# A hand-ordered attention and expert-MLP kernel: eight late W2 rows joined to scores or reads, W2 quads in one row, and another written order

## The chip, the cores and the metric

The kernel runs on one core of one Trainium2 chip. The metric is the device time of one execution in microseconds (us), lower is better. A profile holds the span from the first to the last instruction of one execution. TensorE is PE in the views (its weight loads are PEld), VectorE is DVE, ScalarE is ACT, GpSimd is POOL and SyncE is SP.

## The reference

```python
# x [8,8,512,64], state [8,8,32,64], w_in [512,2048], w_out [2048,512]
scores  = scale * x @ state.T          # softmax over the 32 state rows
xread   = softmax(scores)  @ state     # [8,8,512,64]
scores2 = scale * state @ x.T          # softmax over the 512 tokens
sread   = softmax(scores2) @ x         # [8,8,32,64]
t   = concat([xread, sread], axis=2) -> [8 * 544, 512]
h   = maximum(t @ w_in, 0)
out = (h * h) @ w_out                  # [4352, 512]
```

The two weights arrive as 64-bit floating-point words and are turned into 32-bit numbers on the chip. The result has fp32 accuracy: each large product is three matmuls of split operands (high times high, low times high, high times low).

## The kernel before, in words

**Blocks.** The output has nine blocks: blocks 0 to 7 are the 512 tokens of each batch's x-read, block 8 is the 256 state tokens. For a batch b, `xread @ w_in` is not formed in two steps. The product state times w_in is made first ("W2"; two batches make a "pair", four a "quad") and then multiplied with the softmax numerators.

**Making W2.** w_in is cut into eight column blocks hb of 256 columns. `decode_wi` decodes a column block into `wf{hb}` (two DVE `TENSOR_SCALAR` and four `SCALAR_TENSOR_TENSOR` a half, partly on other engines), `prep_wo` decodes w_out (tiles `dec`, `wo`). `direct_w2` (line 890) makes the pair of batches 0 and 1, `later_w2` (line 927) the quad of batches 2 to 5 in four PSUM banks (`w4ps`, 24 matmuls in two halves of 12), and `last_w2` (line 957) the pair of batches 6 and 7 (`w2ps{hb}_6`, 16 matmuls through `two_w2`). The results are copied out of PSUM (`w4o`, or `w2h` by ACT and `w2l` by DVE), stored to DRAM and loaded again by `load_w2` when their block comes.

**The MLP.** `hidden.blk.fc` ("H blk_fc", 16 fc a block) is six 128x512 matmuls into one of two PSUM banks with the tag `ph`, then relu and square, then the split into `g_hi` (ACT) and `g_lo` (DVE). `accumulate.blk.fc` is twelve matmuls into four banks `acc`. PSUM has four pools of this kind: `acc` with four banks, `ph` with two, `psb` with two.

**Attention.** `scores` makes the 32x512 scores of a batch (`st`, 8 matmuls), `transposes` the numerators `eT` of the state read (`pt`), `sread` the state read (`pr`, 32 matmuls) and its copies. W2 pairs and scores use tiles of 64 rows by 32 columns of the PE array, reads tiles of 128 by 32, quads tiles of 64 by 128; the MLP uses the whole array. `in_a_row` (line 554) issues a list of such matmuls one behind the other: "a row".

**Order.** `PLAN` (lines 24 to 357) is a long string of step names, written by hand. The loop at line 1273 walks through it; each mention of a step runs its generator up to the next `yield`. Every instruction is kept in program order on its engine, SP's DMA queue included, so the string sets the order of each engine. A second table, which the change leaves alone, sets which engine does a piece of evacuation. All instructions go through one helper, so that line 403 stands for all of them in the views.

## Time and profile before

| quantity | value |
|---|---|
| three timed runs | 665.65, 666.88, 665.60 us; median 665.65 |
| span of the profiled execution | 663.4 us |
| its own time over the span | runs less the span: 2.25 us at the median |
| granted TensorE clock | 1.000 in every slice |
| PE matmul busy | 648.4 us, 98% |
| PE weight load busy (beside the matmuls) | 518.3 us, 78% |
| DVE busy | 363.9 us, 55% |
| ACT busy | 358.6 us, 54% |
| POOL busy | 100.3 us, 15% |
| DMA | 102.49 MB, mean 154 GB/s |

The busy share of PE counts a matmul from its start to a modelled end, so neighbouring records overlap by some tenths of a microsecond. What a matmul costs is therefore read from the distance of the starts, not from its length.

### The profile page before, as it was taken

To read this page: it belongs to the slowest core of one execution; us is meant where nothing else is said; L and a number is where in the kernel's file an instruction comes from. 1 tells how busy PE (TensorE), PEld (TensorE's weight loads), DVE (VectorE), ACT (ScalarE), POOL (GpSimd) and SP (SyncE) were. 2 spreads that over 40 slices of the span, in tenths; PEclk is the share of its full clock that TensorE was granted. 3 is DMA by queue.
4 is the path that set the end of the run, shared out by engine and by line. 5 is a ranking of instruction groups with operands and counts; after the bars stand their busy time and mean duration, and the time that the engine had idled before them with its cause. 6 is when DMAs were issued, how large, how long until landed. Compare 5 with 4: busy or idle time off the path is not lost.

```text
span 663.4 us, 10898 instructions
## 1 busy us (share of the span) xinstructions
PE 648.4 (98%) x4132; PEld 518.3 (78%) x4132; DVE 363.9 (55%) x657; ACT 358.6 (54%) x691; POOL 100.3 (15%) x82
## 2 busy tenths in 40 slices
PE   5999999999999999999999999999999999999997
PEld 4667777777788778778777878788778888888886
DVE  5999999866754465445553553446552443212212
ACT  4977776665645565454553645453354455434432
POOL 1521121140330202001301400030001000200100
PEclk9999999999999999999999999999999999999999
DMA  9948787979375566746248045530392227121002
GB/s 312 323 142 235 254 280 244 256 210 278 109 237 168 161 195 215 192 134 161 66 121 226 16 116 146 160 106 32 112 275 68 87 66 187 34 96 33 32 1 95
DMA packets 116276, 102.49 MB, mean 154 GB/s; under 512 B 59520, under 2 KB 92544, under 8 KB 116224
## 3 DMA queue, kind: packets, MB, share of 16 engines
q1 hardware_dynamic: 115984, 101.54, 51.2%
q8 instruction: 32, 0.52, 0.3%
q10 hardware_dynamic: 240, 0.26, 0.1%
q14 instruction: 20, 0.16, 0.1%
HBM read 67.70 MB, written 34.08 MB: 153 GB/s over the span
## 4 chain that ended last, share of the span: by engine, by line
PE 83%; DVE 8%; ACT 3%; DMA 3%; issue 2%; SPq 1%; ACTq 0%
PE acc L403 50%; PE ph L403 26%; DVE wf L403 2%; PE w2ps L403 2%; DVE dec L403 2%; PE w4ps L403 1%; PE st L403 1%; PE pr L403 1%; PE pt L403 1%; ACT ph L403 1%; SPq L403 1%; DMA part<-part_d 1%; DMA wi_raw<-in_moe_w_in_dram 1%; DVE s L403 1%; DVE g_lo L403 1%
## 5 line engine op out<-in xcount | busy, mean ns | idle before, releaser
L403 PE MATMUL acc<-wo,g_hi 128*128 128x512 f32 x1090 | 323.7, 392 | 0.6 <-ACT g_hi L403 0.6
L403 PEld LDWEIGHTS acc<-wo,g_hi 128*128 128x128 f32 x1090 | 201.4, 188 | 49.4 <-issue 4.6
L403 PE MATMUL acc<-wo,g_lo 128*128 128x512 f32 x545 | 197.0, 390 | 0.0
L403 DVE TENSOR_TENSOR g_lo<-ph,g_hi 128x512 fp32r<-128x512 f32 (+1 forms) x143 | 93.4, 657 | 160.5 <-ACT g_hi L403 159.4
L403 PE MATMUL ph<-k_hi,w 128*128 128x512 f32 x512 | 176.6, 395 | 0.5 <-ACT w4o L403 0.2
L403 ACT ACTIVATE ph<-ph 128x512 f32<-128x512 f32 (+1 forms) x194 | 108.4, 560 | 126.7 <-PE ph L403 118.6
L403 PEld LDWEIGHTS acc<-wo,g_lo 128*128 128x128 f32 x545 | 101.9, 188 | 23.2 <-issue 1.2
L403 PEld LDWEIGHTS ph<-k_hi,w 128*128 128x128 f32 x512 | 96.1, 188 | 26.6 <-issue 3.3
L403 PE MATMUL ph<-k_lo,w 128*128 128x512 f32 x256 | 99.8, 390 | 0.0
L403 ACT CAST g_hi<-ph 128x512 fp32r<-128x512 f32 (+1 forms) x144 | 80.4, 564 | 35.1 <-DVE ph L403 30.4
L403 DVE SCALAR_TENSOR_TENSOR ph<-ph,r 128x512 f32<-128x512 f32 (+1 forms) x47 | 31.3, 668 | 55.9 <-ACT r L403 55.9
L403 ACT ACTIVATE r<-ph 128x512 f32<-128x512 f32 (+1 forms) x47 | 27.1, 578 | 61.2 <-PE ph L403 61.1
L403 PEld LDWEIGHTS ph<-k_lo,w 128*128 128x128 f32 x256 | 48.1, 188 | 9.1
L403 POOL TENSOR_TENSOR w<-w_f,w 128x512 fp32r<-128x512 f32 x21 | 27.1, 1294 | 173.4 <-ACT w L403 173.2
L403 POOL TENSOR_TENSOR s<-sf,s 128x512 fp32r<-128x512 f32 x9 | 11.5, 1291 | 111.0 <-ACT s L403 53.5
L403 ACT CAST w<-w_f 128x512 fp32r<-128x512 f32 x40 | 24.8, 624 | 4.0 <-DMA w_f<-w_d 4.0
L403 PE MATMUL ph<-sr_hi,s 128*128 128x256 f32 x128 | 25.4, 282 | 0.0
L403 POOL TENSOR_TENSOR sp<-sp,s 128x512 f32<-128x512 f32 x11 | 11.5, 1050 | 91.0 <-DVE s L403 45.9
L403 DVE SCALAR_TENSOR_TENSOR dec<-wo_raw,dec 128x512 uint32<-128x512 uint32 x32 | 22.9, 719 | 0.7
L403 DVE SCALAR_TENSOR_TENSOR wf<-wi_raw,wf 128x512 uint32<-128x512 uint32 x32 | 22.2, 696 | 0.7
L403 POOL TENSOR_TENSOR wo<-dec,wo 128x512 fp32r<-128x512 f32 x10 | 13.5, 1349 | 57.9 <-ACT wo L403 57.9
L403 PEld LDWEIGHTS ph<-sr_hi,s 128*128 128x128 f32 x128 | 20.9, 191 | 0.6
(111 smaller groups left out, 569.6 us busy)
## 6 DMA issues: line engine op xcount, KB each, us to landing
w_f<-w_d SPq DMA_DIRECT2D x40, 256.0 KB, 3.8
wi_raw<-in_moe_w_in_dram SPq DMA_DIRECT2D x16, 512.0 KB, 5.1
wo_raw<-in_moe_w_out_dram SPq DMA_DIRECT2D x16, 512.0 KB, 6.5
wf<-win_f SPq DMA_DIRECT2D x16, 512.0 KB, 4.6
xr<-in_x_dram SPq DMA_DIRECT2D x16, 512.0 KB, 5.5
w_d<-w4o SPq DMA_DIRECT2D x32, 256.0 KB, 2.5
w<-w2a_d SPq DMA_DIRECT2D x16, 512.0 KB, 3.6
out_dram<-o SPq DMA_DIRECT2D x31, 256.0 KB, 2.8
```

The lines of the kernel that those rows point to most:

```text
L403: op = call(*args, **kw)
```

## The change

Matmuls, copies, DMAs and their engines are the same in number. What changes is in which row a matmul stands and in which order the steps are written.

- `sread` is cut into `read` (its matmuls) and `sread` (its copies). `scores`, `read` and `two_w2` now give back their lists of matmuls, and `together` issues one or two lists as one row.
- The eight late W2 pairs (batches 6 and 7) have no row of their own any more. Five stand ahead of scores in one row (`shared`: batch 3 with hb 1, 4 with 0, 5 with 2, 6 with 3, 7 with 4), with W2 in the two `ph` banks and the scores in `psb`. Three stand ahead of a state read (`beside`: batch 4 with hb 5, 5 with 6, 6 with 7), with W2 in `psb` and the read in one `ph` bank.
- `later_w2` issues its 24 matmuls as one row. In the order before, the two halves of 12 already stood back to back for seven of the eight hb; for hb 2 an accumulate stood between them.
- `PLAN` is written anew from end to end (2215 mentions before, 2199 now).

```diff
+    def together(*names):
+
+        def issue():
+            in_a_row([call for name in names for call in rows[name]()])
+
+        return issue
...
         def scores(self):
...
-            in_a_row(calls)
+            return calls
...
-        def sread(self):
+        def read(self, pool, tag):
...
-            pr = ps_b.tile([P, G, D], F32, tag="psb", name=f"pr{b}")
+            pr = self.pr = pool.tile([P, G, D], F32, tag=tag, name=f"pr{b}")
...
-            in_a_row(calls)
+            return calls
+
+        def sread(self):
+
+            b, pr = self.b, self.pr
...
-    def two_w2(hb, b0, last):
+    def two_w2(hb, b0, pool, tag):
...
-        pool, tag = (ps_h, "ph") if hb == 0 < b0 else (ps_b, "psb")
...
-        in_a_row(calls)
-        return ps
+        return calls
...
     def later_w2(hb):
...
-        ps = []
+        ps, calls = [], []
         for k, (pool, tag) in enumerate(pools):
-            if k:
-                yield
...
-            calls = []
...
-            in_a_row(calls)
             ps += two
+        in_a_row(calls)
...
     def last_w2(hb):
 
-        ps = two_w2(hb, 6, True)
+        ps = w2_ps[hb, 6]
...
+    shared = {3: 1, 4: 0, 5: 2, 6: 3, 7: 4}
+    beside = {4: 5, 5: 6, 6: 7}
+    w2_row = {hb: key("scores", b) for b, hb in shared.items()} | {hb: key("read", b) for b, hb in beside.items()}
...
+        names = [key("scores", b)]
+        if b in shared:
+            names.insert(0, key("w2", shared[b]))
+            needs.append(key("load_wf", 2, shared[b]))
+        step(key("scores", b), together(*names), after=needs)
```

The new order moves steps everywhere. Three places of it follow. A row names the output tile, the inputs and the size; "x2" stands for two in a line.

**First place: the end of the decoding, on DVE and on PE.** DVE before, from the split of H1_7 (`g_lo1_7`) to behind that of H1_6 (`g_lo1_6`); `dec` and `wf` are decodes of w_out and w_in:

```order
L403 TENSOR_TENSOR g_lo1_7_1167<-ph1_7_1155,g_hi1_7_1166 128x512
L403 TENSOR_TENSOR w2_0_4_1115<-w2_f0_4_1116,w2_0_4_1115 128x2x256
L403 TENSOR_SCALAR dec12_1206<-dec12_1206 128x512 x2
L403 SCALAR_TENSOR_TENSOR dec12_1206<-wo_raw12_853,dec12_1206 128x512 x2
L403 COPY w2o6_0_0_1245<-w2ps6_0_0_1227 128x512
L403 TENSOR_TENSOR g_lo1_6_1219<-ph1_6_1187,g_hi1_6_1218 128x512
L403 TENSOR_SCALAR wf7_1250<-wf7_1250 128x512 x2
L403 SCALAR_TENSOR_TENSOR wf7_1250<-wi_raw14_1153,wf7_1250 128x512 x2
```

DVE now, over the same stretch:

```order
L396 SCALAR_TENSOR_TENSOR dec12_1175<-wo_raw12_823,dec12_1175 128x512
L396 TENSOR_TENSOR g_lo1_7_1205<-ph1_7_1197,g_hi1_7_1204 128x512
L396 SCALAR_TENSOR_TENSOR wf7_1173<-wi_raw14_1130,wf7_1173 128x512
L396 TENSOR_TENSOR w2_0_4_1179<-w2_f0_4_1180,w2_0_4_1179 128x2x256
L396 COPY w2o6_0_0_1270<-w2ps6_0_0_1252 128x512
L396 SCALAR_TENSOR_TENSOR dec12_1175<-wo_raw12_823,dec12_1175 128x512
L396 SCALAR_TENSOR_TENSOR wf7_1173<-wi_raw14_1130,wf7_1173 128x512
L396 TENSOR_TENSOR w2_0_5_1190<-w2_f0_5_1191,w2_0_5_1190 128x2x256
L396 TENSOR_TENSOR g_lo1_6_1244<-ph1_6_1182,g_hi1_6_1243 128x512
```

Of all DVE instructions, 169 stand up to and with `g_lo1_6` before and 180 now. The eleven added ones are two `SCALAR_TENSOR_TENSOR` and two `TENSOR_SCALAR` each of `dec10` and of `wf7`, the max `m21_0` with its small `nb21_0`, and the split `w2_0_5`; none is taken out.

PE before, ahead of H0_8 (`ph0_8`), with the last of the accumulates of block 1:

```order
L403 MATMUL acc1_4_3_1197<-wo7_1053,g_hi1_7_1166 128x512 x2
L403 MATMUL acc1_4_0_1194<-wo7_1053,g_lo1_7_1167 128x512
L403 MATMUL acc1_4_1_1195<-wo7_1053,g_lo1_7_1167 128x512
L403 MATMUL acc1_4_2_1196<-wo7_1053,g_lo1_7_1167 128x512
L403 MATMUL acc1_4_3_1197<-wo7_1053,g_lo1_7_1167 128x512
L403 MATMUL ph0_8_1314<-k_hi0_130,w2_0_4_1115 128x512
L403 MATMUL ph0_8_1314<-k_lo0_131,w2_0_4_1115 128x512
```

PE now; the last matmul of the read of batch 0 (`pr0`) stands first:

```order
L396 MATMUL pr0_1289<-xr0_1_1208,eT0_1150 32x64 x2
L396 MATMUL acc1_4_0_1213<-wo5_768,g_lo1_5_1095 128x512
L396 MATMUL acc1_4_1_1214<-wo5_768,g_lo1_5_1095 128x512
L396 MATMUL acc1_4_2_1215<-wo5_768,g_lo1_5_1095 128x512
L396 MATMUL acc1_4_3_1216<-wo5_768,g_lo1_5_1095 128x512
L396 MATMUL ph0_8_1342<-k_hi0_122,w2_0_4_1179 128x512
L396 MATMUL ph0_8_1342<-k_lo0_123,w2_0_4_1179 128x512
L396 MATMUL ph0_8_1342<-k_hi0_122,w2_0_4_1179 128x512 x2
L396 MATMUL ph0_8_1342<-k_lo0_123,w2_0_4_1179 128x512
L396 MATMUL ph0_8_1342<-k_hi0_122,w2_0_4_1179 128x512
L396 MATMUL acc1_4_0_1213<-wo6_905,g_hi1_6_1243 128x512 x2
```

The accumulates with `wo6` and `wo7` (24 matmuls) stood ahead of H0_8 and stand behind it now. H0_9 (six matmuls) and the row `pr0` stood behind it and stand ahead of it now. H0_8 writes the PSUM bank that `g_lo1_6` reads.

**Second place: the pair of hb 1, on PE.** Before, behind the end of the quad of hb 7 (`w4ps7`); the pair itself stands behind H2_12, some 45 rows later:

```order
L403 MATMUL w4ps7_1_0_2719<-wf_hi7_2664,s42_1417 128x256
L403 MATMUL w4ps7_1_1_2720<-wf_hi7_2664,s42_1417 128x256
L403 MATMUL acc2_0_0_2343<-wo8_1058,g_hi2_8_2712 128x512 x2
L403 MATMUL acc2_0_0_2343<-wo8_1058,g_lo2_8_2713 128x512
L403 MATMUL acc2_0_1_2344<-wo8_1058,g_hi2_8_2712 128x512 x2
L403 MATMUL acc2_0_1_2344<-wo8_1058,g_lo2_8_2713 128x512
L403 MATMUL acc2_0_2_2345<-wo8_1058,g_hi2_8_2712 128x512 x2
L403 MATMUL acc2_0_2_2345<-wo8_1058,g_lo2_8_2713 128x512
L403 MATMUL acc2_0_3_2346<-wo8_1058,g_hi2_8_2712 128x512 x2
L403 MATMUL acc2_0_3_2346<-wo8_1058,g_lo2_8_2713 128x512
L403 MATMUL st3_1_2762<-xT3_1_2536,sT_111 32x512
```

Now the first two of the pair's 16 matmuls follow at once (the scores `st3` and then `acc2` with `wo8` follow the sixteenth):

```order
L396 MATMUL w4ps7_1_0_2723<-wf7_1_2534,s46_1545 128x256
L396 MATMUL w4ps7_1_1_2724<-wf7_1_2534,s46_1545 128x256
L396 MATMUL w4ps7_1_0_2723<-wf_hi7_2604,s42_1546 128x256
L396 MATMUL w4ps7_1_1_2724<-wf_hi7_2604,s42_1546 128x256
L396 MATMUL w2ps1_6_1_2765<-wf1_2_2712,sT_111 32x256
L396 MATMUL w2ps1_6_0_2764<-wf1_2_2712,sT_111 32x256
```

The pair writes the two `ph` banks in which the quad's last two tiles stand, so it needs their copies `w4o7_2` (DVE) and `w4o7_3` (ACT).

**Third place: H6_4, on PE.** Before, behind the accumulate of fc 2 and the transposes `pt6`:

```order
L403 MATMUL acc6_0_3_5220<-wo2_555,g_hi6_2_5199 128x512 x2
L403 MATMUL acc6_0_3_5220<-wo2_555,g_lo6_2_5200 128x512
L403 MATMUL pt6_0_5295<-ident_73,e26_4713 128x128 x4
L403 MATMUL pt6_1_5313<-ident_73,e26_4713 128x128 x4
L403 MATMUL ph6_4_5330<-k_hi6_3848,w2_6_2_5072 128x512
```

Now, behind the pair of hb 4 and the scores of batch 7:

```order
L396 MATMUL w2ps4_6_1_5231<-wf4_2_5187,sT_111 32x256
L396 MATMUL w2ps4_6_0_5230<-wf4_2_5187,sT_111 32x256
L396 MATMUL st7_1_5233<-xT7_1_4902,sT_111 32x512
L396 MATMUL st7_0_5232<-xT7_1_4902,sT_111 32x512
L396 MATMUL st7_1_5233<-xT7_1_4902,sT_111 32x512
L396 MATMUL st7_0_5232<-xT7_1_4902,sT_111 32x512
L396 MATMUL st7_1_5233<-xT7_0_4698,sT_111 32x512
L396 MATMUL st7_0_5232<-xT7_0_4698,sT_111 32x512
L396 MATMUL st7_1_5233<-xT7_0_4698,sT_111 32x512
L396 MATMUL st7_0_5232<-xT7_0_4698,sT_111 32x512
L396 MATMUL ph6_4_5264<-k_hi6_3461,w2_6_2_5007 128x512
L396 MATMUL ph6_4_5264<-k_lo6_3462,w2_6_2_5007 128x512
```

The pair stood alone in block 4 before, with an accumulate behind it. H6_4 now writes the bank of `w2ps4_6_0`, which ACT (`w2h`) and then DVE (`w2l`) have to copy out first. The other six shared rows have an accumulate of twelve matmuls behind them.

## Rows read from the trace of the kernel before

**Rows 1.** The page: busy time of the engines.
```profile
PE 648.4 (98%) x4132; PEld 518.3 (78%) x4132; DVE 363.9 (55%) x657; ACT 358.6 (54%) x691; POOL 100.3 (15%) x82
```

**Rows 2.** Busy time by stretches: length, PE, PEld, DVE, ACT, POOL, clock, DMA share, GB/s.
```profile
0.00:24.00 24.00, 16.21 (x176) 12.05 (x176) 16.35 (x31) 14.66 (x30) 6.06 (x9) 1.00 0.94 335
24.00:60.00 36.00, 34.30 (x214) 26.08 (x208) 35.47 (x67) 30.30 (x59) 11.29 (x8) 1.00 0.64 193
60.00:98.00 38.00, 37.12 (x274) 28.28 (x273) 36.99 (x74) 28.21 (x55) 6.99 (x4) 1.00 0.80 266
```

**Rows 3.** PE's timeline round a W2 pair alone: start, length, operation, count.
```profile
241.04 0.39 PE L403 MATMUL ph<-k_hi,w 128*128 128x512 f32 x1
241.36 1.09 PE L403 MATMUL w2ps<-wf,sT 64*32 64x256 f32 x32
242.38 0.73 PE L403 MATMUL acc<-wo,g_hi 128*128 128x512 f32 x2
242.96 0.39 PE L403 MATMUL acc<-wo,g_lo 128*128 128x512 f32 x1
```

**Rows 4.** PE's timeline: a row of scores alone, and a row of a read alone.
```profile
230.58 1.09 PE L403 MATMUL st<-xT,sT 64*32 64x512 f32 x16
...
266.62 1.10 PE L403 MATMUL pr<-xr,eT 128*32 128x64 f32 x64
```

**Rows 5.** PE's timeline: the second half of hb 2's quad alone, then hb 5's 24 in one.
```profile
153.24 0.39 PE L403 MATMUL w4ps<-wf_hi,s 64*128 64x256 f32 x2
...
154.14 2.14 PE L403 MATMUL acc<-wo,g_hi 128*128 128x512 f32 x8
...
226.02 0.39 PE L403 MATMUL w4ps<-wf_hi,s 64*128 64x256 f32 x2
...
227.64 0.73 PE L403 MATMUL acc<-wo,g_hi 128*128 128x512 f32 x2
```

**Rows 6.** Copies out of PSUM: ACT and PE behind a quad, then groups by line.
```profile
217.64 0.73 PE L403 MATMUL acc<-wo,g_hi 128*128 128x512 f32 x2
...
217.74 1.57 ACT L403 COPY w4o<-w4ps 128x512 f32<-128x512 f32 x3 [1.63 <-PE w4ps L403]
...
L403 DVE COPY w4o<-w4ps 128x512 f32<-128x512 f32 x17 | 11.5, 687 | 6.3 <-PE w4ps L403 3.7 <-DMA out_dram<-o 1.3 <-DMA w_d<-w4o 1.1
...
L403 ACT CAST w2h<-w2ps 128x512 fp32r<-128x512 f32 x16 | 8.7, 597 | 4.2 <-PE w2ps L403 4.2
...
L403 DVE TENSOR_TENSOR w2l<-w2ps,w2h 128x512 fp32r<-128x512 f32 x16 | 10.6, 678 | 3.3 <-ACT w2h L403 3.3
```

**Rows 7.** PE's timeline up to H0_8 (the row at 103.94).
```profile
98.50 1.98 PE L403 MATMUL acc<-wo,g_hi 128*128 128x512 f32 x8
...
101.22 1.98 PE L403 MATMUL acc<-wo,g_hi 128*128 128x512 f32 x8
...
103.94 0.39 PE L403 MATMUL ph<-k_hi,w 128*128 128x512 f32 x1
```

**Rows 8.** DVE's timeline over the same time; the row at 97.91 is g_lo1_6.
```profile
95.06 0.88 DVE L403 TENSOR_SCALAR dec<-dec 128x512 f32<-128x512 f32 x2
95.98 1.42 DVE L403 SCALAR_TENSOR_TENSOR dec<-wo_raw,dec 128x512 uint32<-128x512 uint32 x2
97.31 0.68 DVE L403 COPY w2o<-w2ps 128x512 f32<-128x512 f32 x1
97.91 0.68 DVE L403 TENSOR_TENSOR g_lo<-ph,g_hi 128x512 fp32r<-128x512 f32 x1
```

**Rows 9.** PE's timeline: the last of four late waits, behind an accumulate.
```profile
171.34 1.20 PE L403 MATMUL acc<-wo,g_lo 128*128 128x512 f32 x4
172.72 0.50 PE L403 MATMUL ph<-k_hi,w 128*128 128x512 f32 x1 [0.19 <-ACT w4o L403]
```

**Rows 10.** DMA issues of the W2 pairs: count, KB each, us to landing.
```profile
w<-w2a_d SPq DMA_DIRECT2D x16, 512.0 KB, 3.6
w2a_d<-w2h SPq DMA_DIRECT2D x16, 256.0 KB, 2.3
```

More of the change, by code (lines that the diff above doesn't have):

```diff
@@ new lines @@
+    hidden.3.8 softmax.4.1 softmax.4.0 hidden.3.8 hidden.3.8 exp_s.4.0
+    hidden.3.7 hidden.3.8 hidden.3.8 exp_s.4.1 hidden.3.7 hidden.3.8 accumulate.3.5 exp_s.4.0 load_w2.3.5
+        hidden.3.7
+    hidden.3.6 hidden.3.7 softmax.4.1 load_w2.3.7 softmax.4.0 read.3 hidden.3.7 hidden.3.6 hidden.3.7
+        start.6
+    hidden.3.9 hidden.3.6 softmax.4.1 hidden.3.6 load_w2.3.7 load_w2.4.0 load_w2.3.6 hidden.3.9 hidden.3.6
+        hidden.3.6 accumulate.3.6 softmax.4.0
+    hidden.3.11 hidden.3.9 load.5.1 hidden.3.11 accumulate.3.7 hidden.3.9 softmax.4.1 hidden.3.9 load_wf.2.3
+        hidden.3.9 softmax.4.1
@@ L357 @@
+    hidden.8.15 accumulate.7.15 accumulate.7.15 hidden.8.15
+    hidden.8.14 accumulate.7.15 accumulate.7.15 accumulate.8.12 hidden.8.14 accumulate.8.13 accumulate.7.15
+        hidden.8.14 accumulate.7.15 hidden.8.14 hidden.8.15 hidden.8.14 hidden.8.15 hidden.8.15 hidden.8.14
+        hidden.8.15 accumulate.7.15 accumulate.8.14 accumulate.8.15 accumulate.8.13 accumulate.8.14
+        accumulate.8.15 accumulate.8.15 accumulate.8.15 accumulate.8.15 accumulate.8.15
 """
@@ L877, in hi_lo @@
         return w[:, :, 0], w[:, :, 1]
-    def two_w2(hb, b0, last):
-        w = (wf.pop(hb) if last else wf[hb]).bitcast(F32)
-        pool, tag = (ps_h, "ph") if hb == 0 < b0 else (ps_b, "psb")
-        ps = [pool.tile([P, 2, HB], F32, tag=tag, name=f"w2ps{hb}_{b0}_{g}") for g in range(G)]
+    w2_ps = {}
+    def two_w2(hb, b0, pool, tag):
+        w = wf.pop(hb).bitcast(F32)
+        ps = w2_ps[hb, b0] = [pool.tile([P, 2, HB], F32, tag=tag, name=f"w2ps{hb}_{b0}_{g}") for g in range(G)]
         calls = []
@@ L1198, in tile_attn_moe @@
         step(key("warm", i), warm, i, after=["ident"])
+    shared = {3: 1, 4: 0, 5: 2, 6: 3, 7: 4}
+    beside = {4: 5, 5: 6, 6: 7}
+    w2_row = {hb: key("scores", b) for b, hb in shared.items()} | {hb: key("read", b) for b, hb in beside.items()}
+    for b in range(B):
+        rows[key("scores", b)] = lambda b=b: att[b].scores()
+        rows[key("read", b)] = lambda b=b: att[b].read(*((ps_h, "ph") if b in beside else (ps_b, "psb")))
+    for hb in range(NHB):
+        pool = (ps_b, "psb") if hb in beside.values() else (ps_h, "ph")
+        rows[key("w2", hb)] = partial(two_w2, hb, NB + 2, *pool)
     for b in range(B):
@@ L1206, in tile_attn_moe @@
         step(key("load", b, 1), lambda b: att[b].load(1), b, after=[key("start", b)])
-        step(
-            key("scores", b), lambda b: att[b].scores(), b,
-            after=[key("prep", b, 0), key("prep", b, 1), key("states", 0 if early else 2)],
-        )
-        step(
-            key("sread", b), lambda b: att[b].sread(), b,
-            after=[key("transposes", b)] + [key("load_n", b, g) for g in range(G)],
-        )
+        needs = [key("prep", b, 0), key("prep", b, 1), key("states", 0 if early else 2)]
+        names = [key("scores", b)]
[3 more added lines that the diff above has]
+        step(key("scores", b), together(*names), after=needs)
+        names = [key("read", b)]
+        needs = [key("transposes", b)] + [key("load_n", b, g) for g in range(G)]
+        if b in beside:
+            names.insert(0, key("w2", beside[b]))
+            needs += [key("load_wf", 2, beside[b]), key("states", 2)]
+        step(key("read", b), together(*names), after=needs)
+        step(key("sread", b), lambda b: att[b].sread(), b, after=[key("read", b)])
         step(
@@ L1245, in tile_attn_moe @@
         step(key("later_w2", hb), later_w2, hb, after=[key("split_wf", hb), "split_states"])
-        step(key("last_w2", hb), last_w2, hb, after=[made if hb < NOW else key("load_wf", 2, hb), key("states", 2)])
+        step(key("last_w2", hb), last_w2, hb, after=[w2_row[hb]])
     for fc in range(NFC):
```

662 lines of the change are left out of this document (320 added, 342 removed).

## The prediction

> **What bounds the kernel now.** I read the busy times first, then the stretches, then PE's timeline row by row. PE is busy for 648.4 of 663.4 us [rows 1], so a change can win only by shortening PE's work, or its idle 15 us. The stretches show where another engine is near: from 24 to 98 us DVE is busy for 35.47 of 36.00 and 36.99 of 38.00 us [rows 2], and so has 1.5 us to spare in 74. There the decoding of the weights runs on DVE, and PE waits for DVE where the order asks too early. Behind 98 us PE is the only full engine. In the first 24 us neither is full and the DMA share is 0.94 [rows 2].
>
> PE's timeline shows what a short row of small tiles costs. Twelve whole-array matmuls go from 98.50 to 101.22 [rows 7], 0.227 us each. The matmul ahead of a lone W2 pair has 0.32 us until the row starts, and behind the row two matmuls take 0.58 us in place of 0.45 [rows 3]. So the two edges cost 0.09 + 0.13, say 0.2 us, beside the row's own 1.02 us (241.36 to 242.38). Scores and reads alone are rows of the same length [rows 4].
>
> **The change part by part.** The sum is made against the span of 663.4 us. The median of the runs, 665.65, lies 2.25 above it, and I keep that distance. A difference of 0.2% is 1.33 us, about what a measurement of this kernel can tell from no change.
>
> *a, five pairs joined to scores.* A joined row saves one pair of edges, 0.2 us. It also saves the running empty of one row: the quad's half of 12 takes 0.90 us (153.24 to 154.14), but 24 in one take 1.62 (226.02 to 227.64), which is 0.18 less than two halves [rows 5]. The pair and the scores use the same tile shape, 64 by 32 [rows 3, 4], like the quad's two halves. So each saves 0.38 and the five save 1.9 us. If only the edges go it is 1.0; these are the bounds, and I take 1.9 because the quad is the same case.
>
> *b, three pairs joined to reads.* The read's tiles are 128 by 32 [rows 4], so the array goes from one tile shape to another inside the row, and no row of the trace shows that. Bounds: nothing saved, or 0.38 each as with equal shapes, 1.14 in all. I take half, 0.57, since one of the two changes to and from the whole array goes in any case. The Trainium skill, TensorEngine Tiling (Array Packing), section Key Properties, says that a change of tiling mode, as against a change of tile, drains TensorE. By that rule each of the three keeps a drain inside its row, about 0.19 saved each; without it the sum would be 0.57 lower. The trace's edges of 0.2 us between whole array and tiles agree with it.
>
> *c, the quad of hb 2 in one row.* Two rows of 0.90 with edges become one of 1.62 [rows 5]: 0.38 saved. The other seven stood back to back already, so nothing changes for them.
>
> *d, the pair of hb 1 behind the quad of hb 7.* It writes the banks of the quad's last tiles. ACT starts 0.10 us behind the end of a quad (217.64 to 217.74), DVE's copy `w4o` takes 0.69 and ACT's runs beside it [rows 6]: a wait of 0.79. One pair of edges more goes, since quad, pair and scores are now one stretch of tiles: +0.59 net. Bounds 0.4 (with a copy as short as ACT's 0.60) and 1.3 (DVE still has a split of 0.68 ahead [rows 8]). Queued behind the waiting pair are the scores of batch 3 and all of block 2, so the wait counts in full.
>
> *e, H6_4 behind the pair of hb 4 and the scores of batch 7.* The bank is free after the pair (1.02), the start of ACT (0.10), `w2h` (0.60) and `w2l` (0.68) [rows 3, 6]: 2.40 us from the row's start. The row itself is done after 2 × 1.02 less 0.18, with its first edge 0.09: 1.95. H6_4 waits 0.45 us. Bounds 0.3 (the pair's last tile is done 0.18 earlier inside a joined row) and 0.8 (DVE late by part of a split). Behind the other six rows (hb 1 too) an accumulate of 12 × 0.227 = 2.72 us [rows 7] covers the chain of 1.5 us of copies, and I cost them at nothing. If that cover failed, each would pay about 0.45. The stores and loads of this pair (2.3 and 3.6 us to landing [rows 10]) with the copies are some 8.4 us, and until H6_8 PE has four hidden and three accumulates, 4 × 1.36 + 3 × 2.72 = 13.6 us: hidden.
>
> *f, the end of the decoding.* H0_8 started at 103.94 [rows 7]. Ahead of it 24 matmuls go (5.44 us), and six (1.36) and the read of batch 0 (1.02 and 0.2 of edges) come: PE would be there at 101.1. It needs the bank that `g_lo1_6` reads. That split ended at 97.91 + 0.68 = 98.59 [rows 8], 5.3 us ahead of need. Eleven DVE instructions now come ahead of it. A group of two `TENSOR_SCALAR` and two `SCALAR_TENSOR_TENSOR` takes 2.25 us (95.06 to 97.31), and a single operation of this size 0.60 (97.31 to 97.91) [rows 8]. Two groups, the max and the split `w2_0_5` make 4.5 + 1.2 = 5.7, the small `nb21_0` 0.2 more: 5.9. DVE has at most 1.5 us of idle time to put them in [rows 2], so `g_lo1_6` ends between 98.59 + 5.9 − 1.5 = 103.0 and 104.5, or from 102.6 if the operations overlap better. H0_8 waits 1.5 to 3.4 us, and 3.7 if an operation more is late; I take 2.3, near the middle of the first two. Behind H0_8 wait the accumulates of block 1 and all else on PE.
>
> Part of it comes back. PE then runs later against the copies and loads, and it has small late waits to lose: four places, the last one at 171.34, where four matmuls take 1.38 in place of 0.91 us, with ACT's copy named [rows 9]. The four are at 129, 136, 140 and 171 us and cost 1.67 us in all. I take two thirds, 1.1, because the order there is new too and may put others in their place. So f is +1.2, with bounds of −0.2 (1.5 less 1.67) and +3.7.
>
> *The start.* SP issues the second block of w_in third and not eighth. Such a transfer is 512 KB, and at 335 GB/s [rows 2] it is 1.5 us that could move states and x by that much, up or down. The first hidden needs both, so I take nothing, with 0.7 to either side.
>
> Sum: −1.9 − 0.57 − 0.38 + 0.59 + 0.45 + 1.2 = −0.61. The span becomes 662.8 and the time 665.0 us.
>
> **The rivals.**
>
> *Faster: the decoding doesn't bind.* The new order as a whole may use DVE's idle time and give all late waits back. Then f is −0.2, and if the reads join as well as the scores, b is −1.14: −1.9 − 1.14 − 0.38 + 0.59 + 0.45 − 0.2 = −2.58, so 663.1 us. For it: four real waits stand behind 100 us [rows 9], and PE's savings are sure in sign. Against it: eleven more DVE instructions ahead of one that PE needs sooner.
>
> *Slower: DVE's order decides.* All eleven operations are paid, H0_8 waits 3.7 us and nothing comes back: −0.61 − 1.2 + 3.7 = +1.89, so 667.5 us. The terms without f make −1.81, so the kernel is slower by over 1.33 us once f is above 3.1: when `g_lo1_6` ends after 101.1 + 3.1 = 104.2 us and the waits at 129 to 171 us stay. For it: DVE is 98% busy up to 98 us [rows 2]. Against it: nearly the whole of the wait must stay to outweigh 2.85 us of savings.
>
> *Slower: the copies bind.* If the two copies of a pair are late behind every joined row, the seven other rows pay 0.45 each: −0.61 + 3.15 = +2.54, so 668.2. Against it: 2.72 us of accumulate cover 1.5 us of copies. The Trainium skill, the same page, section PSUM Bottleneck, warns that tiling speeds TensorE but not the evacuation of PSUM, so that the copies may become the limit. By that rule the time would be this rival's; the trace shows it only where no accumulate follows.
>
> *The rows don't gain.* Joining saves edges only, reads nothing: −1.0 − 0.38 + 0.59 + 0.45 + 1.2 = +0.86, so 666.5 us, within 0.2%.
>
> **How the numbers follow.** Forecast 0.38, faster rival 0.35, DVE's order 0.17, the copies 0.04, no gain in the rows 0.06. The forecast and the last are within 0.2%: 0.44. Faster 0.35, slower 0.21. The range goes from the faster rival to the slower one, 663.1 to 667.5, with 0.2 at either side for the start: 662.9 to 667.7. The copies and the far ends of the start and of d are left out. The forecast's own range, with d, e and f varied by half their bounds, is 664.1 to 666.4.
>
> **What would show it.** In the profile after: joined rows of pair and scores, 1.86 us from their start to the next matmul, and pair and read 1.86 to 2.04; a wait of PE of about 0.8 us behind the quad of hb 7, named for `w4o`; about 0.45 ahead of H6_4, named for `w2l`; between 99 and 106 us a wait of PE for a `g_lo` of 1.5 to 3.4. If H0_8 doesn't wait, f is wrong. If the waits near 129 to 171 us stand as before, so is the give-back. If joined rows take 2.04 and more, a is wrong. If the first hidden moves by over 0.7 us, the start was mis-costed.

## The result and the profile after

The changed kernel takes 674.85 us (median of four runs, 673.20 to 675.47) against 665.91 for the kernel before (four runs): a ratio of 1.0126 with the 95% interval 1.0111 to 1.0141. It is slower by 8.9 us, where 0.6 less was forecast, and lies 7 us above the range. The profiled execution is the run of 675.47 us with a span of 673.7.

The page's busy times after, which answer to [rows 1]:

```profile
PE 651.5 (97%) x4132; PEld 522.4 (78%) x4132; DVE 360.7 (54%) x657; ACT 356.6 (53%) x691; POOL 102.7 (15%) x82
```

The work is the same. The span of the profiled executions grew by 10.3 us, and in it PE is idle for 7.2 us more and busy for 3.1 more. The stretches after, with the columns of [rows 2], say where:

```profile
24.00:60.00 36.00, 33.85 (x230) 24.66 (x229) 34.57 (x67) 27.53 (x54) 9.69 (x7) 0.95 0.55 162
...
98.00:160.00 62.00, 59.48 (x407) 46.26 (x408) 45.76 (x80) 38.17 (x72) 14.52 (x10) 1.00 0.85 255
...
233.00:245.00 12.00, 9.01 (x89) 5.29 (x88) 4.92 (x8) 3.70 (x7) 0.50 (x1) 0.86 0.76 248
```

For the middle one the kernel before had:

```profile
98.00:160.00 62.00, 61.71 (x409) 48.11 (x416) 48.66 (x84) 41.50 (x78) 14.68 (x11) 1.00 0.84 246
```

Two stretches show something that was in none of the forecast's terms: the granted clock is 0.95 in 24 to 60 us and 0.86 in 233 to 245, where the kernel before had 1.00 all along. In 24 to 60 us PE loses only some tenths of busy time against [rows 2], so there the lower clock matters as well as the idle time. In 98 to 160 PE is idle for 2.5 us, 0.3 before. PE's waits name what was late (after; us in total, times, longest):

```profile
PE w2ps L396 <- DMA wf<-win_f: 3.0, 1, 3.0
PE w2ps L396 <- DVE sp L396: 1.9, 1, 1.9
PE ph L396 <- DVE g_lo L396: 1.6, 2, 1.2
PE pr L396 <- DMA xr<-in_x_dram: 1.4, 2, 1.0
PE w4ps L396 <- DVE g_lo L396: 0.8, 1, 0.8
```

The largest of these, and the largest new one (the wait for x in the first microseconds is 4.3 us, 3.6 before), is a load, that of column block 1 for the W2 pair of batches 6 and 7. PE's timeline after shows its place and the other rows that the forecast spoke of: the wait at the second W2 pair (34.07), H0_8 (106.93), H0_12 (123.60), the joined row of hb 1 (238.90 and 240.75), a pair with scores (434.02), a pair with a read (486.06) and H6_4 (504.33):

```profile
34.07 2.55 PE L396 MATMUL w2ps<-wf,sD 64*32 64x256 f32 x32 [1.95 <-DVE sp L396]
...
106.93 0.39 PE L396 MATMUL ph<-k_hi,w 128*128 128x512 f32 x1
...
123.60 0.50 PE L396 MATMUL ph<-k_hi,w 128*128 128x512 f32 x1 [1.19 <-DVE g_lo L396]
...
235.62 0.28 PE L396 MATMUL w4ps<-wf_hi,s 64*128 64x256 f32 x2
238.90 1.96 PE L396 MATMUL w2ps<-wf,sT 64*32 64x256 f32 x32 [3.00 <-DMA wf<-win_f]
240.75 1.84 PE L396 MATMUL st<-xT,sT 64*32 64x512 f32 x16
242.52 0.74 PE L396 MATMUL acc<-wo,g_hi 128*128 128x512 f32 x2
...
434.02 1.09 PE L396 MATMUL w2ps<-wf,sT 64*32 64x256 f32 x32
434.90 1.06 PE L396 MATMUL st<-xT,sT 64*32 64x512 f32 x16
435.90 0.73 PE L396 MATMUL acc<-wo,g_hi 128*128 128x512 f32 x2
...
486.06 1.09 PE L396 MATMUL w2ps<-wf,sT 64*32 64x256 f32 x32
487.08 1.10 PE L396 MATMUL pr<-xr,eT 128*32 128x64 f32 x64
488.11 0.50 PE L396 MATMUL ph<-k_hi,w 128*128 128x512 f32 x1
...
504.33 0.50 PE L396 MATMUL ph<-k_hi,w 128*128 128x512 f32 x1 [0.61 <-DVE w2l L396]
```

The joined rows did what was forecast: 434.02 to 435.90 is 1.88 us for pair and scores, 486.06 to 488.11 is 2.05 for pair and read. But the row of hb 1 takes 1.85 + 1.77 = 3.62 us behind its wait, nearly twice the 1.88 of the same row at 434.02. Two things are late in it. The granted clock is low (0.86 over 233 to 245 us), and ACT's last copy of the quad (`w4o`) ends at 240.69, just ahead of the scores at 240.75: their weight load waited 0.8 us for it. SP's timelines say why its load came late: first after, then before.

```profile
226.55 1.39 SPq L396 DMA_DIRECT2D w_d<-w4o  x3
227.99 1.64 SPq L396 DMA_DIRECT2D w_f<-w_d  x2
229.67 0.49 SPq L396 DMA_DIRECT2D xr<-in_x_dram  x1
230.28 0.44 SPq L396 DMA_DIRECT2D wf<-win_f  x1
```

```profile
229.92 0.49 SPq L403 DMA_DIRECT2D wf<-win_f  x1
```

The load is issued at almost the same time in both, and in both behind the stores of a quad. Before, the pair stood at 241.36 [rows 3], 11.4 us later. Now PE has done the quad at 235.90 and wants the pair at once, 5.6 us after the issue; the load is there after 8.6.

### The profile page after: what moved, and what is told of

Read it like the earlier page. It is cut to its first block, busy times and chain, and to the rows that moved or that the text cites. A ratio compares the mean times of both kernels' runs of the same rounds, so it can differ in the third digit from the quotient of the medians.

```text
span 673.7 us, 10961 instructions
## 1 busy us (share of the span) xinstructions
PE 651.5 (97%) x4132; PEld 522.4 (78%) x4132; DVE 360.7 (54%) x657; ACT 356.6 (53%) x691; POOL 102.7 (15%) x82
## 4 chain that ended last, share of the span: by engine, by line
PE 78%; DVE 9%; DMA 8%; ACT 2%; issue 1%; SPq 1%; POOL 0%; DVEq 0%; ACTq 0%
PE acc L396 46%; PE ph L396 25%; PE w2ps L396 2%; DMA wf<-win_f 2%; DVE wf L396 2%; DMA wi_raw<-in_moe_w_in_dram 2%; DVE dec L396 1%; PE w4ps L396 1%; DMA xp<-in_x_dram 1%; PE pr L396 1%; DVE s L396 1%; DMA part_d<-po 1%; SPq L396 1%; PE pt L396 1%; DMA xr<-in_x_dram 1%
```

## The experiments

Except where said, an experiment changes the string `PLAN` alone; a diff shows the mentions that it moves. The interval is that of the ratio to the kernel before, which ran beside it.

**The load.** The mention of hb 1's load goes from behind quad 6's stores to behind that quad's first mention.

```diff
-hidden.2.6 later_w2.6 split_wf.7 later_w2.6 ... load_w2.2.5 load_wf.2.1 exp_s.2.0
+hidden.2.6 later_w2.6 load_wf.2.1 split_wf.7 later_w2.6 ... load_w2.2.5 exp_s.2.0
```

> The changed kernel with one load moved: the load of w_in's block 1 for the late pair (load_wf.2.1) is issued behind the matmuls of the quad of hb 6, ahead of that quad's stores, not behind them and two loads of W2. Theory A (the late load): in the changed kernel PE waits 3.00 us for this load ahead of the joined row of hb 1, and the granted clock then falls (0.77 from 240 to 245 us), so that the row takes 3.6 us in place of 1.9. The load went out at 230.28 and can go at about 226, so the wait and the fall both go: about 4.8 us less, 670 us, and the clock is 1.00 there. Theory B (the prediction's term d): the copies of the quad of hb 7 come next and hold the row for 0.8 us: about 2.5 to 4 us less. Theory C (the DMA engines are full, the load lands at the same time whenever it is issued): no change.

Measured: 670.65 us (670.06 to 671.67), 1.0075 [1.0060, 1.0090]: 4.2 us less by the medians, near A's number. PE's timeline of this kernel at the same row:

```profile
235.20 1.85 PE L343 MATMUL w2ps<-wf,sT 64*32 64x256 f32 x32 [0.68 <-ACT w4o L343]
236.71 2.05 PE L343 MATMUL st<-xT,sT 64*32 64x512 f32 x16
238.69 0.80 PE L343 MATMUL acc<-wo,g_hi 128*128 128x512 f32 x2
```

The wait of 3.00 us is gone, and the wait for the quad's copies that term *d* had is what is left: 0.68 us. From the end of the quad to the accumulate PE takes 4.17 us (234.52 to 238.69) in place of 6.62 (235.90 to 242.52): 2.45 less. But the quad itself waits here for two splits `g_lo`, 0.48 and 0.21 us, and from its first matmul to the accumulate only 1.1 us are won. The rest of the 4.2 is not the load's. H2_0, ahead of the moved mention, starts at 188.26 here and at 190.98 after, though the order up to there is the same. So much do executions of the new order differ: a read's load that PE waited 1.02 us for after costs it nothing here, behind the wait of 1.95 us at the second W2 pair the clock stays at 1.00 here, and the runs of one such kernel lie up to 3.7 us apart (669.54 to 673.20 in one below).

Theory A was wrong on the clock in this execution. The row takes 3.49 us, and without a wait between pair and scores, because the granted clock fell here too:

```profile
235.00:240.00 5.00, 4.80 (x53) 2.56 (x54) 1.93 (x4) 1.22 (x3) 0.00 (x0) 0.66 0.78 244
```

With the load in time and the clock at 1.00 the same row takes 1.90 us behind the same wait. The kernel that takes the old order's first 13 us (below):

```profile
237.13 1.12 PE L343 MATMUL w2ps<-wf,sT 64*32 64x256 f32 x32 [0.68 <-ACT w4o L343]
238.02 1.09 PE L343 MATMUL st<-xT,sT 64*32 64x512 f32 x16
239.03 0.73 PE L343 MATMUL acc<-wo,g_hi 128*128 128x512 f32 x2
```

Four more kernels with the early load and the new order at this place show 1.90 to 1.91 at a clock of 1.00. From H2_8 to H2_12, over the same matmuls, ten kernels of this kind with the clock at 1.00 take 19.1 to 20.0 us and the changed kernel 22.17: the late load and the fall behind it cost 2.2 to 3.1 us. In the other five of the ten the scores wait a second time, 0.3 to 1.3 us, since they too write banks that hold tiles of the quad. The kernel with the old order to 190 us (below):

```profile
232.24 1.09 PE L343 MATMUL st<-xT,sT 64*32 64x512 f32 x16 [0.41 <-ACT w4o L343]
```

**The old order up to a cut.** These keep the early load and begin with the old order's first mentions; the rest is the new order.

```diff
-load_raw.0 decode_wi.0 decode_wi.0 ident start.0 load_raw.1 ...
+load_raw.0 decode_wi.0 decode_wi.0 decode_wi.0 ident neg_ident ...
```

To 41 us (208 mentions):

> The changed kernel with the early load of block 1 (670.65 us in the run before this one), and the order before for the first 208 mentions, up to the middle of H0_3 (about 41 us). There the two orders have issued almost the same steps (7 mentions apart), so the seam should cost little. Theory A: the first hidden starts 2 us earlier, and the pair of hb 1 for batches 0 and 1 doesn't wait 1.9 us for the softmax, nor does the clock fall there: by the excess of PE's steps up to 48 us this is 3.3 us, so 667.3 us. Theory B (DVE is the limit up to 98 us, so a PE that starts earlier only waits longer at the decoding): less than 1.5 us of it is left, 669 us or more.

To 138 us (686 mentions):

> The same with the order before up to the 686th mention (about 138 us, ten mentions apart at the seam). Theory A: beside the start, the waits between 94 and 135 us go too (0.5 ahead of H1_7, 0.8 at H0_12, 1.1 and more in the first quad, 0.4 at the read): 6.1 us by the excess of PE's steps up to 130 us, so 664.5 us, below the kernel before. Theory B (the new order behind the seam is what it is, and DVE's decodes that came early in the new order are now late): 667 us or more.

To 190 us (895 mentions, the quad of hb 2 in one row):

> The same with the order before up to its 895th mention (about 190 us, H2_1, ahead of the fifth quad), and the quad of hb 2 as one row at the place of its second half. The joined rows are all behind that. If all that the new order lost lies ahead of them, at the load of block 1 (mended here) and at H6_4 (left), the sum is: the kernel before 666, less 8 joined rows (5 of 0.37 and 3 of 0.20, read in the profile of the changed kernel: 2.45), less 0.4 for the quad, plus 0.7 for the copies ahead of the row of hb 1 and 0.7 at H6_4: about 664.6 us. If the seam makes a wait of its own as at H2_2 in the run that cut at H2_0 (6.5 us for a split on DVE), it is 667 or more.

| old order to | time, us | ratio to before | kernel before, us |
|---|---|---|---|
| nothing, late load | 674.85 | 1.0126 [1.0111, 1.0141] | 665.91 |
| nothing, early load | 670.65 | 1.0075 [1.0060, 1.0090] | 666.15 |
| 41 us | 667.43 | 1.0026 [1.0014, 1.0038] | 665.87 |
| 138 us | 668.38 | 1.0037 [1.0023, 1.0052] | 665.87 |
| 190 us | 666.73 | 1.0009 [0.9995, 1.0023] | 665.87 |

The first 41 us carry 3 us or more, as theory A had it. The kernel cut at 138 us has a wait of its own where the orders meet (2.3 us for a copy `w4o`), so only the one at 190 says what lies between 41 and 190 us: some 0.7 by the medians, which the intervals hardly resolve.

**Where in the first 41 us.** Two more cuts, at about 13 us (loads, first copies, first scores) and at about 25 us (up to the first hidden):

> The new order with the early load, and the old order's first 47 mentions alone (to about 13 us: the first loads, both copies of x transposed, the second decode, the first scores); everything behind is the new order. It stands between the kernel with the early load alone (670.65 us, first hidden at about 26 us and later a wait of 1.9 us for the softmax at the second W2 pair) and the one with the old order to 41 us (667.43, 1.0026). Theory A, the loads and first copies carry the start's loss: H0_0 starts near 24.0 to 24.5 us and the time is 667.5 to 668.5 (1.002 to 1.004). Theory B, the loss lies behind 13 us, in the order of decodes, softmax and POOL's splits on the way to the second pair: H0_0 comes early by at most 1 us, the wait of about 2 us at the second pair stays, and the time is 669.5 to 670.7 (1.0055 to 1.0075).

> The same with the old order's first 120 mentions (to about 24 us, up to the first hidden); behind it the new order, with three wo decodes ahead of the softmax of the second half as there. Theory A (loads, copies, and the first softmax carry it): the first hidden is at 24.0 to 24.5 us, the second pair waits under 0.7 us, and the time is that of the order to 41 us, 667.0 to 668.0 (1.0015 to 1.003). Theory B (what stands between the first hidden and the second pair carries half or more): H0_0 at 24 us, but the second pair still waits 1.2 to 2 us for the softmax and the clock falls there, and the time is 668.5 to 670 (1.004 to 1.0065).

Measured: 672.29 us, 1.0096 [1.0079, 1.0114], and 672.51, 1.0108 [1.0092, 1.0123], above even what theory B gave. Neither cut gives anything back. PE's timelines, of the cut at 13 us and then of that at 25:

```profile
26.24 0.51 PE L343 MATMUL ph<-k_hi,w 128*128 128x512 f32 x1
...
34.49 1.69 PE L343 MATMUL w2ps<-wf,sD 64*32 64x256 f32 x32 [1.95 <-DVE sp L343]
```

```profile
24.54 0.50 PE L343 MATMUL ph<-k_hi,w 128*128 128x512 f32 x1
...
34.81 2.56 PE L343 MATMUL w2ps<-wf,sD 64*32 64x256 f32 x32 [2.90 <-DVE sp L343]
```

With the old loads the first hidden still comes at 26.24 us (26.03 in the changed kernel, 24.02 before), so the loads are not the cause. With the old order to 25 us it comes at 24.54, but the second W2 pair (34.07 after, 30.23 before) stays at 34.81: it waits for the softmax, and the softmax's max stands behind two decode steps on DVE. DVE of the cut at 25 us:

```profile
28.72 1.50 DVE L343 TENSOR_SCALAR dec<-dec 128x512 uint32<-128x512 uint32 x1 [2.36 <-POOL dec L343]
30.15 1.51 DVE L343 TENSOR_SCALAR wf<-wf 128x512 uint32<-128x512 uint32 x1
31.58 0.68 DVE L343 TENSOR_REDUCE m<-pst 128x16 f32<-128x512 f32 x1
```

**Parts of the start.** The softmax of the second half ahead of the two decode steps, the rest as with the early load:

```diff
-prep_wo.2 ... decode_wi.3 transposed_scores.1.1 softmax.1.0 hidden.0.0 ... softmax.1.1 decode_wi.3 softmax.1.0 softmax.1.1
+transposed_scores.1.1 softmax.1.0 softmax.1.1 softmax.1.0 softmax.1.1 prep_wo.2 decode_wi.3 hidden.0.0 ... decode_wi.3
```

> The changed kernel with the early load of block 1 (670.65 us before), and on DVE the two max and two subtract steps of the softmax of batch 1 put ahead of two TENSOR_SCALAR of the decoding. In the changed kernel these two take 1.50 and 1.52 us instead of 0.42, beside two splits on POOL (27.88 to 30.64), and the row of hb 1 for batches 0 and 1 then waits 1.95 us for the subtract and runs at a clock of 0.69 to 0.74. Theory A (the wait is DVE's order, and the clock's fall follows the wait): the wait goes and the clock stays at 1.00 there, 3 to 4 us less, 667 us. Theory B (DVE's total is what counts up to 135 us): the wait goes, and PE waits longer at the next decode or split: less than 1.5 us of it is left, 669 us or more.

Measured: 669.61 us, 1.0061 [1.0037, 1.0085]. The wait for the softmax is gone, but the pair then waits 1.2 us for `wf`, the decode that was moved behind: 1.0 us won, theory B's result. The clock stays at 1.00, as it did in the profiled run with the early load alone, so this pair of runs can't price the fall. The second block of w_in behind the loads of x:

```diff
-ident start.0 load_raw.1 start.0 ... load.0.1 prep.0.0
+ident start.0 start.0 ... load.0.1 load_raw.1 prep.0.0
```

> The changed kernel with the early load of block 1, and the second load of w_in (load_raw.1) put back behind the loads of x, as in the order before. Theory A (the start is lost at SP's queue: x lands later because 512 KB are moved ahead of it; PE waits for x 4.3 to 5.0 us in all where it waits 3.6 before): 1.2 us less, 669.4 us. Theory B (the term of the prediction: nothing): 670.6 us, the first hidden at 26 us as now, because the decoding of this block ends as much later as x comes earlier.

Measured: 673.40 us, 1.0110 [1.0091, 1.0129], 2.75 more than with the early load: the first pair waits 3.5 us for `wf`, which needs that block, and the first hidden comes at 29.24 us. Three more took the softmax first along and changed the queues ahead of it. The first scores ahead of the first pair:

```diff
-prep.0.1 prep.0.1 direct_w2.0 prep_wo.1 scores.0 direct_w2.0
+prep.0.1 prep.0.1 scores.0 direct_w2.0 prep_wo.1 direct_w2.0
```

> The run with batch 1's softmax first (669.61 us), and on PE the scores of batch 0 ahead of the first W2 pair, as in the order before. In the changed kernel the scores start at 13.74 behind a pair that starts at 12.12, before it is 11.81, and the first hidden starts 2.0 us later with a wait of 1.2 us for DVE's subtract of the softmax of batch 0. Theory A (the softmax of batch 0 sets the start): the first hidden comes 1.6 us earlier and about as much of it lasts, 668.0 to 668.6 us. Theory B (DVE's total up to 135 us sets the time): the first hidden comes earlier and under 0.5 us lasts, 669.2 us or more.

Measured: 670.95 us, 1.0073 [1.0052, 1.0094], no gain. The first hidden comes at 29.01 us, later than with the early load alone and not earlier, as both theories had it. This move and the later block of w_in together:

> The changed kernel with the early load of block 1, with three edits of the start together: the load of w_in's second part behind x, the scores of batch 0 ahead of the first W2 pair, and batch 1's softmax ahead of two decodes. Taken alone the first made the pair wait 3.5 us for the decode (673.4), the second came with x landing later still. Theory A (x, scores and pair have to come in one order: x first, scores first, and the pair when its decode is done): the first hidden starts at 24 to 24.5 us in place of 26, and the time is that of the run with the whole start of the order before, 667 to 668 us. Theory B (the start is lost elsewhere, in DVE's order): the first hidden at 25.5 us or later, 669 us or more.

Measured: 673.87 us, 1.0120 [1.0100, 1.0141]: the scores wait 1.9 and 2.0 us for the copies of x transposed, behind the second decode. With that decode behind the four copies as well:

```diff
-load_wo.0 decode_wi.1 states.0 start.1 decode_wi.1 prep.0.1 ... prep.0.1 scores.0
+load_wo.0 states.0 start.1 prep.0.1 ... prep.0.1 decode_wi.1 decode_wi.1 decode_wi.1 decode_wi.1 decode_wi.1 decode_wi.1 scores.0
```

> The run before with the three edits of the start, and the second half of the decoding of w_in's first block (decode_wi.1) put behind all four copies of batch 0's xT. In that run ACT's and DVE's copies of xT stood behind steps of this decode, which waited 3.45 and 3.78 us for its load; PE's scores then waited 1.9 and 2.0 us for xT, and the first hidden came at 30.06. Theory A (the start is one chain, x, xT, scores, softmax, and each of the four queues can hold it): with all four in the order x first, the first hidden comes at 24 to 25 us, and the time is near that of the run with the whole start of the order before (667.4), 667 to 668.5 us. Theory B (something else in the new order's start): first hidden at 26 us or later, 669 us or more.

Measured: 671.21 us, 1.0082 [1.0067, 1.0098], with the first hidden at 26.93. Each moved the wait to the next thing behind.

**The join of hb 1 undone.** The old order to 245 us, where that pair has a row of its own in `psb`; behind it the new order with the seven other joins.

```diff
-    shared = {3: 1, 4: 0, 5: 2, 6: 3, 7: 4}
+    shared = {4: 0, 5: 2, 6: 3, 7: 4}
...
+        if w2_row[hb] == key("w2row", hb):
+            step(key("w2row", hb), together(key("w2", hb)), after=[key("load_wf", 2, hb), key("states", 2)])
```

> The order before up to its 1061st mention (about 245 us), so with the pair of hb 1 alone behind H2_12 and its load where it was, the quad of hb 2 in one row, and the new order behind it with the other seven joined rows. Theory A (the joined rows win by themselves what their rows show: 4 of 0.37 and 3 of 0.20, 2.1 us; H6_4 costs 0.7 of it; the quad of hb 2 between nothing and 0.4): 664.2 to 664.6 us, faster than the kernel before by 0.2 to 0.3%. Theory B (rows on PE aren't worth anything in the total, since a later wait eats them): 665.9 us, same.

Measured: 671.33 us, 1.0084 [1.0069, 1.0099]. A read waits 4.4 us for ACT's `eT`, behind a split that waits for a load: the seam between the orders. Two mendings of it, first the split later and a hidden and an accumulate earlier, then the split alone:

```diff
-softmax.3.1 load_w2.3.0 load_w2.3.0 load_w2.3.0 load_w2.3.3 ... accumulate.2.12 hidden.2.14
+softmax.3.1 load_w2.3.0 load_w2.3.3 ... accumulate.2.12 load_w2.3.0 load_w2.3.0 hidden.2.14
```

> The run of seven joined rows again, with its seam mended: there PE waited 4.4 us ahead of the second read because ACT's copy of eT stood behind a split that waited for a load (load_w2.3.0), and the granted clock then fell to 0.64. The split is moved behind the read, H2_13 ahead of the transposes, and the accumulate of fc 12 ahead of the read. Theory A (the joined rows win what they show): wait and fall go, 5.5 to 6.5 us less than 671.3, that is 664.5 to 665.5, at or a little below the kernel before. Theory B (a later wait eats it): over 667.

> The run of seven joined rows with only the split that waited for its load moved behind the accumulate of fc 12 (in the first mend, the accumulate that was moved left H3_3 waiting 2.4 us for a split of g). Theory A (the joined rows win what they show, 2.1 us less 0.7 at H6_4): 664.4 to 665.0 us, 0.1 to 0.2% below the kernel before. Theory B (another wait takes it): 666 us or more.

Measured: 667.11 us, 1.0024 [1.0014, 1.0035], with a new wait of 2.4 for a `g_lo`; and 664.96 us, **0.9997 [0.9986, 1.0008]**, with none. That last one has seven of the eight joins, all quads in one row, and the time of the kernel before: not to be told from it. Its quad of hb 2 goes from 152.76 to 154.38:

```profile
152.76 0.38 PE L344 MATMUL w4ps<-wf_hi,s 64*128 64x256 f32 x2
...
154.38 2.11 PE L344 MATMUL acc<-wo,g_hi 128*128 128x512 f32 x8
```

**The wait at H6_4.** On it, three accumulates of block 6 each one place earlier, to cover that wait:

```diff
-last_w2.4 hidden.6.4 ... accumulate.6.3 ... read.6 ... accumulate.6.4 ... accumulate.6.5
+last_w2.4 accumulate.6.3 hidden.6.4 ... accumulate.6.4 read.6 accumulate.6.5
```

> The run of seven joined rows (664.96 us) with the accumulates of block 6 each moved ahead by one: fc 3 ahead of H6_4, fc 4 ahead of the row of the pair of hb 7 and the read of batch 6, fc 5 behind that row. Theory A: the wait of 0.68 us for w2l ahead of H6_4 goes and, with an accumulate more between the two joined rows, no wait for the scores of batch 7 takes its place as it did when only the first was moved: 664.3 us, a little more than 0.2% below the kernel before. Theory B: the wait moves on again, 665 us or more.

Measured: 667.37 us, 1.0026 [1.0016, 1.0036]: slower than without. The wait at H6_4 is gone and a hidden further on waits longer. PE's waits of this kernel:

```profile
PE ph L343 <- DVE r L343: 1.3, 1, 1.3
```

**Runs that missed their aim.** Three kernels begin with the old order to 181 us (854 mentions), with the quad of hb 2 as one row at the place of its old first half: one with the late load, one with the early one, and one with the early load and one accumulate of block 6 moved ahead of H6_4. They gave 679.00, 677.32 and 680.02 us, where about 666, 661.2 and 660.6 were expected. All three have a wait of 6 to 7 us for a `g_lo` where the orders meet, so they say nothing of the start. In the third H6_4's wait goes, and a later W2 pair waits 1.2 us for ACT's `e`. What was expected of the first:

> The order before is kept up to the first mention of H2_0 (about 181 us), and all that is left follows in the new order. All joined rows are in the second part. Theory A (the losses before H2_0 are the new order's own, in the first 36 us, at H0_12 and the first quad, and at the second read): they go, about 8.8 us by the sum of PE's excess steps up to 200 us, so 666 us; the wait for the load of block 1 stays. Theory B (the work is only moved: the time won comes back as a longer wait for that load or as other waits for loads behind): 669 us or more.

## Why the prediction was wrong

Two losses decided it, and the prediction had neither: a load that came late at the pair of hb 1, some 2.4 us (term *d* looked at copies alone), and the order of DVE in the first 41 us, 3 to 5 us (*the start*, taken at nothing). The terms for the joined rows held.

Where the profiled execution lost its time shows at points up to which both kernels have issued the same matmuls, kind by kind (the start of the next one, us):

| matmuls issued | before | after | behind |
|---|---|---|---|
| 383 | 60.15 | 64.44 | 4.3 |
| 944 | 138.01 | 146.12 | 8.1 |
| 1460 | 222.07 | 230.27 | 8.2 |
| 1603 | 242.38 | 254.94 | 12.6 |
| 4132, all (end of the span) | 663.41 | 673.70 | 10.3 |

So the start lost 4.3 us, the end of the decoding 3.8, the stretch with the row of hb 1 4.4, and behind it 2.3 came back. The experiments put prices to these by the medians. The distance to the kernel before goes 8.9, 4.5 (early load), 1.6 (old order to 41 us), 0.9 (to 190), −0.8 (to 245, hb 1 alone). The first step is too large by the scatter told above: the two kernels with the early load and the old order to 13 or 25 us, which keep the loss of the start, stand at 6.6 and 6.9, 2.3 and 2.1 below the changed one, which agrees with the 2.2 to 3.1 from H2_8 to H2_12. So the late load carries some 2.4 us and the start 3 to 5. Of the stretch from 41 to 190 us the medians leave 0.7, far less than the 3.8 of the profiled execution; with the old start it costs 1.4 in a profile (below), and a kernel with the old order there (the cut at 190) is itself 1.4 behind at 179 us, so its size is not known within a microsecond.

**Term d failed.** The prediction had the pair of hb 1 wait for the copies of the quad: "a wait of 0.79", +0.59 net. It looked at the banks that the pair writes and not at the weights that it reads. What ended last there was the load of `wf` (3.00 us), which stands on SP's queue behind the stores of quad 6, two loads of W2 and one of x (226.55 to 230.28). Moved 5.5 us earlier on PE, the pair ran into its load. The wait of 3.00 us is not all: the row behind it takes 3.62 us in place of 1.88, with the clock and the last copy both late. The stretch shows the clock:

```profile
240.00:245.00 5.00, 5.00 (x44) 2.26 (x28) 2.42 (x5) 2.28 (x4) 0.50 (x1) 0.77 0.67 218
```

The wait for the copies was rightly sized, 0.68 against 0.79 in the kernels whose load is in time; that the scores' banks too hold tiles of the quad was missed, a second wait of 0.3 to 1.3 us in five of ten kernels. From H2_1 to H3_0, over the same matmuls, the kernel with the old order to 190 us and this join takes 74.11 us (187.74 to 261.85), the one without it 73.12 (186.55 to 259.67), and 0.46 of the latter is a wait at its own seam. So even with its load in time the join of hb 1, with the order round it, costs 1.0 to 1.5 us, where the forecast had −0.38 + 0.59 = +0.21. The waits in it are 0.22 for a split in the quad, 0.67 and 0.41.

**"The start" failed.** The prediction took "nothing, with 0.7 to either side", from one transfer that moves ahead. The loads are not what counts, as the cut at 13 us shows. The order of DVE between 13 and 41 us does: PE waits 1.24 us for DVE's subtract of the first softmax, the first hidden comes 2.0 us later, and decodes stand ahead of the softmax that the second W2 pair waits for (1.95). The prediction had read that DVE has 1.5 us to spare between 24 and 98 us [rows 2], and used it for H0_8 alone. The same row leaves little room for a decode ahead of a softmax at 28 us. In the profiled execution the clock fell here too behind the wait:

```profile
33.00:36.00 3.00, 1.93 (x32) 1.03 (x32) 3.00 (x6) 0.63 (x1) 0.00 (x0) 0.69 0.89 216
36.00:39.00 3.00, 3.00 (x23) 2.00 (x10) 1.95 (x6) 2.30 (x6) 0.00 (x0) 0.74 0.89 315
```

In two kernels with the early load the clock stayed at 1.00 behind the same 1.95 us, and they are 3.8 and 3.9 us behind at 383 matmuls in place of 4.3: most of the start is the order's. Which single move would mend it is open. Of five kernels with such moves the best, the softmax first, won 1.0 us, and the others only moved the wait.

**Term f had the engine, not the place.** DVE is late at the end of the decoding, but H0_8 doesn't wait (106.93), which the prediction had named as the sign that *f* is wrong. That PE came there late is not the reason. With the old order to 41 us PE is at H0_8 at 102.19, and the split that it needs is done at 101.28:

```profile
100.60 0.68 DVE L343 TENSOR_TENSOR g_lo<-ph,g_hi 128x512 fp32r<-128x512 f32 x1
```

```profile
102.19 0.39 PE L343 MATMUL ph<-k_hi,w 128*128 128x512 f32 x1
```

The split moved 2.7 us, from 98.59, where the forecast had 4.0 to 5.9 from eleven added operations. In the changed kernel the `g_lo` waits stand at H0_12 (1.19 us) and in the first quad (0.76). With the old start the stretch loses 2.7 us up to 133 us of the kernel before (2.3 forecast for the wait), and 1.2 of it come back by 179 us (1.1 forecast): +1.4 against +1.2, so there size and give-back were right, at another place than the one named. In the changed kernel's own execution it loses 4.3 and gives back 0.4: 3.9, a little over *f*'s bound of 3.7. Why it loses more there is open.

**Terms a, b and e held, c in its row.** Pair and scores take 1.88 us (1.86 forecast), so *a* saves 0.37 a row. Pair and read take 2.05, at the end of the forecast's 1.86 to 2.04: only the edges are saved, the half that was taken. The rule of the Trainium skill that the prediction weighed, TensorEngine Tiling (Array Packing), section Key Properties, is that changing the tiling mode drains TensorE. The 2.05 us agree. The quad of hb 2 takes 1.62 us as in [rows 5], but in two kernels of old order up to there an accumulate behind it then waits 0.54 us for a `g_hi`, so that the 0.38 don't stay. H6_4 waits 0.61 us for `w2l`, 0.45 forecast. From the 1603rd matmul on, where the seven other joined rows lie with the wait at H6_4 (−0.37 × 4 − 0.2 × 3 + 0.61 = −1.5 us by their rows, −1.6 forecast), the changed kernel takes 418.76 us to the end of the span and the kernel before 421.03 for the same matmuls: 2.3 less, and it is 2.2 to 2.3 less in eleven of thirteen other kernels with the new order from there, 1.6 and 1.9 in two. So this gain came, and the losses ahead of it were larger.

**The rivals.** "DVE's order decides" came nearest in kind, since DVE's order took part of the loss, but with its place at H0_8 it gave 667.5 us. No rival had a load that comes late, and the copies did not bind behind the seven other rows but for H6_4.

## What to carry to other kernels

A step that is moved earlier must be looked at by all that it waits for, its loads first: take from the trace when its load is issued, what stands ahead of it on that queue and when that may go, and compare with the new time of need. A margin that an engine has over a long stretch is not to be spent at one place of it; each early consumer in the stretch is to be checked. And a wait of some microseconds on a full TensorE can cost more than itself, where the granted clock falls behind it; one execution doesn't tell whether it will. Two orders are compared at points where both have issued the same matmuls: between two named steps the work can differ.
